# Opening a fused attention and feed-forward kernel in quarters instead of halves

## Chip, cores, metric

One core of one Trainium2 chip. The metric is the device time of one execution in microseconds (us).

## The reference, cut to what matters

```python
mod = (silu(c) @ w_mod).reshape(1, 6, 1, 1024)
sa, ca, ga, sb, cb, gb = (mod[:, i] for i in range(6))
h = layernorm(x) * (1 + ca) + sa                 # x: 2048 tokens x 1024
x = x + ga * attention(h, k_cache, v_cache, wq, wo)   # 32 query heads of 128
h = layernorm(x) * (1 + cb) + sb
x = x + gb * swiglu(h, w_gate, w_up, w_down)
```

The opening computes `q = h @ wq` for the first heads and the first 512 tokens. It needs the *scale columns* (the part of `w_mod` that gives `ca`, 2 MB), the first 512 columns of `wq` (four heads, 1 MB), and 512 normalised tokens, transposed. The shift `sa` enters later, as a bias on `q`.

## The kernel before: the parts concerned

P = 128, DT = 8 contraction tiles, HK = 4, CH = 512 tokens. Every load goes through SyncE's queue in this order:

```python
def load_wca(hf):                      # scale columns, one half: rows of 512 columns = 1024 B
    for i in range(4):
        SP.dma_start(wca[hf][:, 2*i:2*i+2, :], w_mod[2*i*P:(2*i+2)*P, D+hf*512:D+(hf+1)*512] ...)
for hf in range(2):
    load_wca(hf)
    load_wq0(hf)                       # first weights, half of the contraction
load_wq(1)                             # second group of weights (heads 4 to 7), 1 MB
load_k(0); ...shift columns...; load_v(0); load_wq(2)
load_x(1)                              # second 512 tokens, one load of 1 MB
```

The first heads, by halves of the contraction and of the tokens, with scale matmuls (`mod_ca`, one column each) and scaling out of PSUM (`x_mod`) between them:

```python
for kc in range(HK):
    for h in range(3):
        q_first(h, kc, 0, 2 * P)       # 256 tokens
    ...                                # transposes, x_mod, scale matmuls of half 1, other 256 tokens
for kc in range(HK, DT):
    for h in range(4):
        q_first(h, kc, 0, CH)
for h in range(4): q_raw(h)            # to SBUF
qproj_mm(4, QB0[4], 0, DT)             # fifth head: needs the second group of weights
```

Later, in the first turns of attention (`QB`, bank 4, is also the projection's bank; `XB`, bank 7, is free there):

```python
if i == 1: scores(0)
if i in (1, 3, 5): q_bias_mm(i + 1, i + 3, QB)   # ends with a copy out of the bank on VectorE
if i % 2 == 0: qproj(NQ0 - 1 + i // 2)           # writes bank QB
```

In the same turns ScalarE runs exponentials and, between them, statistics of the second 512 tokens (`stats_act`).

The softmax here doesn't subtract the row's maximum and nothing guards it: scores larger than these inputs give would overflow.

## Time and profile before

| | before |
|---|---|
| three runs | 1158.01, 1158.25, 1160.08 |
| span of the profiled run | 1156.8 |
| TensorE busy | 1145.8 (99%) |
| first projection starts | 11.29 |
| second group of weights lands, 15 engines / all 16 | 18.71 / 20.09 |
| fifth head starts | 20.14 |
| second exponential pair starts | 33.78 |

A load is spread over 16 DMA engines and counts as landed when the last has reported. "15 engines" is the landing without the slowest one. The two can differ by more than a microsecond here.

### The profile page before, as it was taken

The numbers are of one execution on the slowest core, as the hardware profiler recorded it, in microseconds if no ns is written. First come the engines' busy times: TensorE is split into PE (matmuls) and PEld (weight loads), VectorE is DVE, ScalarE is ACT, GpSimd is POOL, SyncE is SP. The second block draws the span as 40 slices with busy tenths as digits, with TensorE's granted clock in tenths as the row PEclk, the third lists the DMA queues.
The fourth block names the chain that finished last, engine by engine and source line by source line (L and its number), as shares of the span: only waits on it lengthen the run. The fifth ranks groups of instructions, "written<-read, shape, count | busy, mean of one in ns | idle before, by whom it ended". The sixth has DMA issues, their size and how long they took to land.

```text
span 1156.8 us, 18111 instructions
## 1 busy us (share of the span) xinstructions
PE 1145.8 (99%) x7029; PEld 585.5 (51%) x7029; DVE 825.1 (71%) x1651; ACT 532.0 (46%) x745; POOL 67.6 (6%) x137
## 2 busy tenths in 40 slices
PE   8999999999999999999999999999999999999999
PEld 5555656654446566656444444444444444444444
DVE  4777997747667777786657898777558777776536
ACT  3867787720127777787100354454110444444110
POOL 1100231000000111111000010000000000000000
DMA  9789899986808898945764332423874423234443
GB/s 321 135 178 216 214 211 207 239 188 180 238 16 186 205 209 212 205 96 126 195 198 151 94 88 73 110 74 100 209 206 140 119 76 107 73 98 131 131 159 109
DMA packets 298532, 179.96 MB, mean 156 GB/s; under 512 B 140496, under 2 KB 287696, under 8 KB 298448
## 3 DMA queue, kind: packets, MB, share of 16 engines
q1 hardware_dynamic: 235472, 92.31, 37.3%
q10 hardware_dynamic: 54336, 55.05, 15.2%
q0 software_dynamic: 8640, 31.46, 8.6%
q8 instruction: 55, 0.90, 0.3%
q14 instruction: 29, 0.24, 0.1%
HBM read 125.96 MB, written 19.92 MB: 126 GB/s over the span
## 4 chain that ended last, share of the span: by engine, by line
PE 93%; DMA 2%; DVE 2%; issue 1%; ACT 1%; SPq 1%; DVEq 0%; ACTq 0%
PE ps L272 93%; DMA arena<-in_A_wq_dram 1%; DMA arena<-nsc 1%; DVE arena L826 1%; ACT arena L796 1%; DMA arena<-arena 1%; DVE arena L897 0%; SPq L341 0%; DVE arena L1053 0%; DVE st L417 0%; SPq L310 0%; SPq L359 0%; DVE arena L843 0%; DVE nsc L431 0%; DVE arena L1552 0%
## 5 line engine op out<-in xcount | busy, mean ns | idle before, releaser
L272 PE MATMUL ps<-arena 128*128 128x512 f16 (+2 forms) x6800 | 1140.4, 330 | 7.9 <-POOL arena L410 2.2
L272 PEld LDWEIGHTS ps<-arena 128*128 128x128 bf16 (+1 forms) x6800 | 577.8, 98 | 564.5 <-DVE arena L826 7.0
L796 ACT ACTIVATE arena<-ps 128x1024 bf16<-128x1024 f32 x256 | 261.2, 1021 | 43.7 <-PE ps L272 31.9
L829 ACT ACTIVATE tmp<-ps 128x512 f32<-128x512 f32 x167 | 99.7, 597 | 295.5 <-PE ps L272 284.6
L897 DVE TENSOR_TENSOR arena<-arena 128x512 f16<-128x512 bf16 x328 | 133.1, 418 | 3.0
L826 DVE TENSOR_TENSOR arena<-ps,tmp 128x512 bf16<-128x512 f32 (+1 forms) x134 | 91.7, 685 | 50.7 <-PE ps L272 37.8
L829 ACT ACTIVATE nsc<-ps 128x512 f32<-128x512 f32 x84 | 50.1, 596 | 93.2 <-PE ps L272 90.9
L818 DVE TENSOR_TENSOR arena<-ps,rl 128x512 f16<-128x512 f32 x128 | 88.5, 691 | 5.1 <-DVE rl L815 0.7
L826 DVE TENSOR_TENSOR arena<-ps,nsc 128x512 f16<-128x512 f32 x84 | 57.3, 686 | 41.0 <-PE ps L272 29.7
L815 DVE RECIPROCAL rl<-ps 128x4 f32<-128x4 f32 x128 | 23.0, 180 | 75.6 <-PE ps L272 74.8
L1113 DVE TENSOR_TENSOR tmp<-ps,tmp 128x512 f32<-128x512 f32 x32 | 22.0, 689 | 61.0 <-ACT tmp L829 51.4
L1537 ACT ACTIVATE arena<-arena 128x512 f16<-128x512 f16 x84 | 49.9, 624 | 32.7 <-DVE arena L826 32.7
L1037 DVE TENSOR_TENSOR arena<-arena 128x2048 f16<-128x2048 f16 (+3 forms) x56 | 56.0, 1010 | 9.3 <-PE ps L272 8.8
L829 ACT ACTIVATE arena<-ps 128x512 f32<-128x512 f32 x16 | 9.6, 597 | 90.7 <-PE ps L272 90.7
L947 DVE TENSOR_TENSOR arena<-arena 128x512 f16<-128x512 bf16 x120 | 47.8, 419 | 1.4 <-DMA arena<-in_A_wo_dram 0.4
L417 DVE BATCH_NORM_STATS2 st<-x_res 128x6 f32<-128x512 bf16 x58 | 39.5, 682 | 3.7 <-DMA x_res<-in_A_x_dram 3.4
L594 DVE SCALAR_TENSOR_TENSOR arena<-arena 128x1024 bf16<-128x1024 bf16 x32 | 38.9, 1215 | 0.0
L1552 DVE TENSOR_TENSOR arena<-arena 128x512 f16<-128x512 f16 x84 | 35.0, 416 | 0.3
L1114 DVE TENSOR_TENSOR tmp<-tmp,rowb 128x512 f32<-128x512 f32 (+1 forms) x49 | 33.6, 686 | 1.7
L431 DVE TENSOR_SCALAR nsc<-x_res,mv,rstd 128x1024 f16<-128x1024 bf16 (+1 forms) x30 | 16.2, 538 | 22.3 <-DMA arena<-nsc 21.0
L1115 DVE TENSOR_TENSOR arena<-tmp,x_res 128x512 bf16<-128x512 f32 (+1 forms) x33 | 22.3, 676 | 1.1
L826 DVE TENSOR_TENSOR arena<-ps,rowb 128x512 f16<-128x512 f32 x28 | 19.3, 689 | 3.9 <-ACT rowb L829 3.4
(85 smaller groups left out, 325.6 us busy)
## 6 DMA issues: line engine op xcount, KB each, us to landing
arena<-in_A_wq_dram SPq DMA_DIRECT2D x28, 512.0 KB, 5.1
arena<-wo_sum ACTq DMA_DIRECT2D x7, 2048.0 KB, 8.8
arena<-in_B_w_gate_dram SPq DMA_DIRECT2D x28, 512.0 KB, 4.0
arena<-in_B_w_up_dram SPq DMA_DIRECT2D x28, 512.0 KB, 5.1
arena<-wd_sum ACTq DMA_DIRECT2D x8, 1792.0 KB, 7.8
arena<-in_B_w_down_dram ACTq DMA_DIRECT2D x6, 1792.0 KB, 7.2
arena<-in_A_wo_dram POOLq DMA_DIRECT2D x16, 512.0 KB, 4.9
wo_sum<-arena POOLq DMA_DIRECT2D x16, 512.0 KB, 5.0
```

The costliest lines, as they stand in the source:

```text
L272: T.op(PE, lambda: TE.matmul(out_ap, lhsT, rhs, start=start, stop=stop, skip_group_check=skip), reads=reads, writes=[bank_buf])
L417: T.op(DVE, lambda: V.bn_stats(st_[sl][:, hf * 6:hf * 6 + 6], x_res[:, t, hf * 512:hf * 512 + 512]), reads=[B_x[t]], writes=[B_st[sl]])
L594: T.op(DVE, lambda: V.scalar_tensor_tensor(mt[n % 2], mt[n % 2], 1.0, sc_row, op0=ALU.mult, op1=ALU.mult, accum_out=mcol[:, n:n + 1]), rea ...
L796: T.op(ACT, lambda: A.activation(ex_s[es][:, 2 * kp:2 * kp + 2, :], banks2(SCB + 2 * kp), AF.Exp, scale=att_scale), writes=[PB[SCB + 2 * k ...
L818: T.op(DVE, lambda: V.tensor_tensor(o_s[os_].rearrange("p (a b) d -> p a b d", a=2), psap(PVB * 512, [[512, 2], [130, 2], [1, P]]), rlb, A ...
L826: T.op(DVE, lambda: V.tensor_tensor(out, bank(ba), other, ADD), reads=[ob2], writes=[PB[ba], ob])
L829: T.op(ACT, lambda: A.activation(dst, bank(bk), AF.Copy), writes=[PB[bk], db])
L897: T.op(st, lambda: eng.tensor_tensor(o, a, b, op), reads=rd, writes=[wr])
L947: T.op(DVE, lambda: V.tensor_tensor(o, a, b, SUB), reads=rd, writes=[wr])
L1037: T.op(DVE, lambda: V.tensor_tensor(o, a, b, SUB), reads=rd, writes=[sb])
L1537: T.op(ACT, lambda: A.activation(o, s_, AF.Silu), reads=[sb], writes=[ob])
L1552: T.op(DVE, lambda: V.tensor_tensor(gu[blk][:, p, :], o, s_, MULT), reads=[sb, ob], writes=[B_gu[blk][p]])
```

## The change

Intent: start TensorE's useful work sooner. Scale columns and first weights come two contraction tiles at a time, all four heads take each quarter at once, and each token half gets its own PSUM bank. One later line moves the bias columns to the spare bank.

```diff
-            def load_wca(hf):
-                for i in range(4):
-                    T.op(dq("q_wca%d_%d" % (hf, i)), lambda: SP.dma_start(
-                        wca[hf][:, 2 * i:2 * i + 2, :],
-                        w_mod[2 * i * P:(2 * i + 2) * P, D + hf * 512:D + (hf + 1) * 512] ...
+            def load_wca(q):
+                parts = 2 if q == 0 else 1
+                m = DT // parts
+                for i in range(parts):
+                    T.op(dq("q_wca%d_%d" % (q, i)), lambda: SP.dma_start(
+                        wca[q][:, i * m:(i + 1) * m, :],
+                        w_mod[i * m * P:(i + 1) * m * P, D + q * 2 * P:D + (q + 1) * 2 * P] ...
...
-            for hf in range(2):
-                load_wca(hf)
-                load_wq0(hf)
+            for q in range(NQR):
+                load_wca(q)
+                load_wq0(q)
...
+            def x_place(t, dt):
+                if dt < HK:
+                    return t // 2, dt * 2 * P + t % 2 * P
+                return (0 if dt % 2 else 2), (dt - HK) // 2 * CH + t * P
...
-            warm(12, WB)
+            warm(10, WB)
...
+            q_four(0, 0, 2 * P)
+            mod_ca(1)
+            x_gain(1)
+            x_mod(1, 0, B_hT[0])
+            x_first(2, range(HK))
+            x_first(tl, range(HK))
+            x_mod(0, 2, B_h0b)
+            q_four(1, 0, 2 * P)
...
+            q_four(2, 0, CH)
+            q_four(3, 0, CH)
...
-                    q_bias_mm(i + 1, i + 3, QB)
+                    q_bias_mm(i + 1, i + 3, XB)
```

More of the change, by code (lines that the diff above doesn't have):

```diff
@@ L333, in _ @@
             ND = 12
-            B_wca = [[_Buf("wca%d_%d" % (hf, i)) for i in range(4)] for hf in range(2)]
+            NQR = DT // 2
+            B_wca = [[_Buf("wca%d_%d" % (q, i)) for i in range(2)] for q in range(NQR)]
             B_wsa = [_Buf("wsa%d" % k) for k in range(DT)]
-            wca = [arena.at(OFF_OT[2] + hf * 8 * KB, [DT, 512], BF16, B_wca[hf]) for hf in range(2)]
+            wca = [arena.at(OFF_OT[2] + q * 4 * KB, [DT, 2 * P], BF16, B_wca[q]) for q in range(NQR)]
             wsa = arena.at(OFF_OT[3], [DT, D], BF16, B_wsa)
-            def load_wca(hf):
-                for i in range(4):
-                    T.op(dq("q_wca%d_%d" % (hf, i)), lambda: SP.dma_start(
-                        wca[hf][:, 2 * i:2 * i + 2, :],
-                        w_mod[2 * i * P:(2 * i + 2) * P, D + hf * 512:D + (hf + 1) * 512].rearrange("(k p) n -> p k n", p=P)),
-                         writes=[B_wca[hf][i]])
+            def load_wca(q):
[4 more added lines that the diff above has]
+                        wca[q][:, i * m:(i + 1) * m, :],
+                        w_mod[i * m * P:(i + 1) * m * P, D + q * 2 * P:D + (q + 1) * 2 * P].rearrange("(k p) n -> p k n", p=P)),
+                         writes=[B_wca[q][i]] if parts == 2 else B_wca[q])
             NWQ = 2
@@ L356, in load_wq, with load_wq0 @@
                     wq_s[gidx], A_wq[:, gidx * 512:(gidx + 1) * 512].rearrange("(k p) n -> p k n", p=P)), writes=B_wq[gidx])
-            def load_wq0(kh):
-                T.op(dq("q_wq0%d" % kh), lambda: SP.dma_start(
-                    wq_s[0][:, kh * HK:(kh + 1) * HK, :],
-                    A_wq[kh * HK * P:(kh + 1) * HK * P, 0:512].rearrange("(k p) n -> p k n", p=P)), writes=[B_wq[0][kh]])
+            B_wq0 = [_Buf("wq0_%d" % q) for q in range(NQR)]
+            def load_wq0(q):
+                T.op(dq("q_wq0%d" % q), lambda: SP.dma_start(
+                    wq_s[0][:, 2 * q:2 * q + 2, :],
+                    A_wq[2 * q * P:(2 * q + 2) * P, 0:512].rearrange("(k p) n -> p k n", p=P)), writes=[B_wq0[q]])
             def load_wsa(k2):
@@ L490, in warm @@
                     mm(bank(b), zwarm[:, 0:P], zwarm, True, True, [B_zw], PB[b])
-            def x_first(t, d0=0, n=DT):
-                for dt in range(d0, d0 + n):
-                    o = (dt % 2) * CH + t * P
-                    transpose(bank_bf(dt // 2)[:, o:o + P], nsc4[t][:, dt * P:(dt + 1) * P], [B_ns4[t]], PB[dt // 2])
-            def x_gain(hf):
-                T.op(DVE, lambda: V.tensor_scalar(gain_f[:, hf * HK:(hf + 1) * HK], psap(XB * 512, [[2, HK]]), 1.0, None, op0=ALU.add),
-                     writes=[PB[XB], B_g[0]])
@@ L503, in x_mod @@
-            def x_mod(hf, c0, n, bufs):
-                for dt in (0, 2, 1, 3):
-                    dt += hf * HK
-                    src = bank_bf(dt // 2)[:, (dt % 2) * CH + c0:(dt % 2) * CH + c0 + n]
-                    dst = hT[0][:, dt, c0:c0 + n]
-                    if dt % 4 < 2:
+            B_gq = [_Buf("gq%d" % q) for q in range(NQR)]
+            def x_place(t, dt):
+                if dt < HK:
+                    return t // 2, dt * 2 * P + t % 2 * P
+                return (0 if dt % 2 else 2), (dt - HK) // 2 * CH + t * P
@@ new lines, in x_first, with x_gain, x_mod @@
+            def x_first(t, dts):
+                for dt in dts:
+                    bk, o = x_place(t, dt)
+                    transpose(bank_bf(bk)[:, o:o + P], nsc4[t][:, dt * P:(dt + 1) * P], [B_ns4[t]], PB[bk])
+            def x_gain(q):
+                T.op(DVE, lambda: V.tensor_scalar(gain_f[:, 2 * q:2 * q + 2], psap(XB * 512, [[2, 2]]), 1.0, None, op0=ALU.add),
+                     writes=[PB[XB], B_gq[q]])
+            def x_mod(q, t, bufs):
+                n = 2 * P if q < 2 else CH
+                for dt in (2 * q, 2 * q + 1):
+                    bk, o = x_place(t, dt)
+                    src = bank_bf(bk)[:, o:o + n]
+                    dst = hT[0][:, dt, t * P:t * P + n]
+                    if (t if q < 2 else dt % 2) == 0:
@@ L509, in x_mod @@
                         T.op(DVE, lambda: V.tensor_scalar(dst, src, gain_f[:, dt:dt + 1], None, op0=ALU.mult),
-                             reads=[B_g[0]], writes=[PB[dt // 2], bufs[dt]])
+                             reads=[B_gq[q]], writes=[PB[bk], bufs[dt]])
                     else:
                         T.op(ACT, lambda: A.activation(dst, src, AF.Copy, scale=gain_f[:, dt:dt + 1]),
-                             reads=[B_g[0]], writes=[PB[dt // 2], bufs[dt]])
+                             reads=[B_gq[q]], writes=[PB[bk], bufs[dt]])
@@ L515, in _, with mod_ca @@
             MCOLS = [(j, j) for j in range(DT)]
-            def mod_ca(hf, k):
-                mod_mm(wca[hf][:, k, :], B_wca[hf][k // 2], k, MCOLS[0:HK])
+            def mod_ca(q, k0=0, k1=DT):
+                for k in range(k0, k1):
+                    mod_mm(wca[q][:, k, :], B_wca[q][k // HK], k, MCOLS[0:2])
             WB = PVB
@@ L555, in _ @@
             norm(0, 0, 0)
-            stats_only(2)
+            stats(2, 2, 0)
+            norm(1, 1, 1)
+            stats(2, 2, 1)
+            T.op(DVE, lambda: V.bn_aggr(mv[2][:, :], st_[2][:, :]), reads=[B_st[2]], writes=[B_mv[2]])
             rstd_of(2, mv[2][:, 1:2], B_mv[2], 1.0)
             rstd_of(tl, acc[:, 1:2], B_acc, 1.0 / D)
-            norm(1, 1, 1)
-            norm(2, 2, 2, 0, 512)
-            warm(12, WB)
-            x_first(0)
-            warm(3, WB)
-            for k in range(4):
-                mod_ca(0, k)
-            x_first(1)
-            for k in range(4, DT):
-                mod_ca(0, k)
-                if k == 5:
-                    warm(1, WB)
-            x_first(2, 0, HK)
-            x_gain(0)
-            x_mod(0, 0, 2 * P, B_hT[0])
-            norm_last(0, 512)
-            norm(2, 2, 2, 512, 512)
+            warm(10, WB)
+            x_first(0, range(HK))
+            warm(2, WB)
+            mod_ca(0, 0, HK)
+            warm(1, WB)
+            x_first(1, range(HK))
+            mod_ca(0, HK, DT)
+            x_gain(0)
+            x_mod(0, 0, B_hT[0])
+            x_first(0, (4, 6))
+            x_first(1, (4, 6))
+            norm(2, 2, 2)
+            norm_last(0, D)
             NL = NJ - NE
@@ L653, in _ @@
             BB = SCB + 3
-            QB0 = [QB, PVB, PVB + 1, SCB, SCB + 1, SCB + 2, QB, PVB]
+            QB0 = [QB, PVB, PVB + 1, SCB + 3, SCB + 1, SCB + 2, QB, PVB]
             def q_raw(h):
@@ L696, in q_first @@
                 mm(bank(QB0[h], n, c0), wq_s[0][:, kc, h * P:(h + 1) * P], hT[0][:, kc, c0:c0 + n],
-                   kc == 0 and c0 == 0, kc == DT - 1, [B_wq[0][kc // HK], bufs[kc]], PB[QB0[h]], skip=True)
-            for kc in range(HK):
-                for h in range(3):
-                    q_first(h, kc, 0, 2 * P)
-                if kc == 2:
-                    x_first(tl, 0, HK)
-                    x_mod(0, 2 * P, 2 * P, B_h0b)
-                    norm_last(512, 512)
-            for k in range(4):
-                mod_ca(1, k)
@@ L708, in _ @@
-            x_first(2, HK, HK)
-            for kc in range(HK):
-                for h in range(3):
-                    q_first(h, kc, 2 * P, 2 * P, B_h0b)
-                if kc == 1:
-                    x_first(tl, HK, HK)
-                    for k in range(4, DT):
-                        mod_ca(1, k)
-                    x_gain(1)
-                    x_mod(1, 0, CH, B_hT[0])
-            for kc in range(HK):
-                q_first(3, kc, 0, CH)
-            for kc in range(HK, DT):
-                for h in range(4):
-                    q_first(h, kc, 0, CH)
+                   kc == 0 and c0 == 0, kc == DT - 1, [B_wq0[kc // 2], bufs[kc]], PB[QB0[h]], skip=True)
@@ new lines, in q_four @@
+            def q_four(q, c0, n, bufs=B_hT[0]):
+                for kc in (2 * q, 2 * q + 1):
+                    for h in range(4):
+                        q_first(h, kc, c0, n, bufs)
+            q_four(0, 0, 2 * P)
[6 more added lines that the diff above has]
+            q_four(1, 0, 2 * P)
+            x_mod(1, 2, B_h0b)
+            q_four(0, 2 * P, 2 * P, B_h0b)
@@ L723, in _ @@
+            mod_ca(2)
+            x_gain(2)
+            for t in range(2, TPC):
+                x_first(t, (4, 6))
+            for t in range(TPC):
+                x_first(t, (5, 7))
+            x_mod(2, 0, B_hT[0])
+            q_four(1, 2 * P, 2 * P, B_h0b)
+            mod_ca(3)
+            x_gain(3)
+            x_mod(3, 0, B_hT[0])
+            q_four(2, 0, CH)
+            q_four(3, 0, CH)
             for h in range(4):
                 q_raw(h)
-            T.op(DVE, lambda: V.tensor_copy(gain[0][:, :], gain_f[:, :]), writes=[B_g[0]])
+            T.op(DVE, lambda: V.tensor_copy(gain[0][:, :], gain_f[:, :]), reads=B_gq, writes=[B_g[0]])
```

## The prediction

> **What bounds the kernel now.** I read the page first (busy shares, then the chain that ended last), then the chain and each engine's order of time over the first 60 us, since every changed line but one runs before 20 us, and the last one before 43 us.
>
> ```profile
> PE 1145.8 (99%) x7029; PEld 585.5 (51%) x7029; DVE 825.1 (71%) x1651; ACT 532.0 (46%) x745; POOL 67.6 (6%) x137
> PE 93%; DMA 2%; DVE 2%; issue 1%; ACT 1%; SPq 1%; DVEq 0%; ACTq 0%
> ```
>
> TensorE is busy for 99% and carries 93% of the chain. Its idle time in the whole run is 1156.8 - 1145.8 = 11.0 us, 0.95% of the span, so no opening of any shape gains 2% by removing waits. The chain over the stretch that changes:
>
> ```profile
> 8.60 11.49 DMA arena<-in_A_wq_dram
> 20.09 0.05 issue
> 20.14 2.28 PE ps L272 x24
> ...
> 29.50 1.60 PE ps L272 x20
> 31.10 0.02 issue
> 31.12 0.17 DVE bq L668
> 31.29 0.14 issue
> 31.43 3.44 PE ps L272 x24
> 34.87 0.03 issue
> 34.90 1.03 ACT arena L796
> ```
>
> Columns are start, length, what. Until 20.09 us the chain is not TensorE at all: it is the DMA queue, and its last link is the landing of the second group of query weights (1 MB, issued at 8.60, landed 20.09). From there it is TensorE, with a small detour over VectorE at 31.12 and exponentials on ScalarE later. TensorE's own order of time says how near the two limits lie:
>
> ```profile
> 11.29 1.16 PE L272 MATMUL ps<-arena 128*128 128x256 f16 x9 [0.65 <-DMA arena<-in_A_wq_dram]
> 20.14 1.90 PE L272 MATMUL ps<-arena 128*128 128x512 f16 x8 [0.27 <-DMA arena<-in_A_wq_dram]
> 31.43 1.24 PE L272 MATMUL ps<-arena 128*128 128x512 f16 x5 [0.51 <-DVE bq L668]
> ```
>
> The brackets are idle time before the group and what ended it. The first heads' matmuls start at 11.29, after 0.65 us for the weights' first half; their last one could have been followed by another at about 19.7 (the row before ends at a modelled 19.87), and then TensorE waits for the second group until 20.14. The last line is a separate wait, taken up below.
>
> **The Trainium skill.** "DMA: Bandwidth & Descriptors", Specifications, puts the smallest transfer for line rate at 512 B. The change cuts the scale columns' rows from 1024 B to 512 B, so this matters. This trace has both sizes in saturated stretches of one microsecond; the last number is GB/s:
>
> ```profile
> 10.00:11.00 1.00, 0.64 (x13) 0.37 (x10) 0.70 (x3) 0.26 (x1) 0.58 (x1) 1.00 1.07 358
> 12.00:13.00 1.00, 1.00 (x19) 0.93 (x17) 0.40 (x3) 0.29 (x1) 0.00 (x0) 1.00 1.10 353
> 955.00:956.00 1.00, 1.00 (x6) 0.44 (x5) 0.97 (x4) 0.60 (x1) 0.00 (x0) 1.00 1.15 346
> ```
>
> The first two move 1024 B packets, the third 512 B packets (gate weights): 346 against 353 and 358, so it agrees nearly, with a few per cent lost. "Runtime: NRT & Kernel Launch", Instruction fetch mechanics, says that a sequencer fetches its own program in 16 KiB blocks of 256 instructions by its own DMA queue. The trace agrees: the page's
>
> ```profile
> q8 instruction: 55, 0.90, 0.3%
> ```
>
> is 55 packets of 16384 B, and TensorE's 14,058 weight loads and matmuls make 54.9 blocks of 256. "PSUM — Partial Sum Buffer", bank collisions, says two engines may not touch one bank at once, so programs guard by bank and not by address; this kernel's waits do that, as the 0.51 us above shows: the next projection and the two bias columns being copied lie in one bank. "TensorE: Matmul & The Clock Gate" gives a floor of about 25 ns from start to start for small matmuls; the 16 one-column matmuls at 12.83 start 25 ns apart, so splitting them by quarters costs nothing as long as their number stays.
>
> **The change part by part.**
>
> *Loads ahead of the second group.* Bytes are equal: tokens 1 MB, scale columns 2 MB, first weights 1 MB. Only their order and the 512 B rows differ. First matmul: before, 1 MB of scale columns and 0.5 MB of weights had to land (11.24); now 0.5 and 0.25 MB. The last tokens landed at 6.69 and a 256 KB piece took about 0.75 us, so three pieces are in at about 9.0, some 2 us earlier. The second group's landing cannot profit, since the same bytes are queued before it: 2.10 MB at 340 instead of 355 GB/s is 6.17 - 5.91 = 0.26 us later.
>
> That landing has a second part. In the trace 15 of its 16 engines' completions were in by 18.71 and the last at 20.09: one DMA engine is 1.38 us late in everything from then on. At 15.75 a 16 KB instruction block (1127 ns) was fetched, when TensorE had started 141 matmuls. In the new order the 141st falls in the last quarter's scale matmuls (my count: 128 before them), about 16.2, still before the group has drained. So I expect the same lateness: 20.09 + 0.26 = about 20.35.
>
> *TensorE's work to the first four heads.* Transposes 32 both times; scale matmuls 64 both; projections 24 of 256 columns and 20 of 512 become 32 and 16, the same columns (16,384, at 216 ns per 512: 6.9 us); warming matmuls 18 become 15 in all. I walked the new order with durations of this trace (statistics 0.69, normalising 0.49, 256 columns from PSUM 0.35 on VectorE and 0.48 on ScalarE, 512 columns 0.48 and 0.69, power on POOL 0.55): second normalisation 8.2 instead of 8.97; first gain 9.3; first projection 9.8; two gaps, about 0.7 us before it and 0.35 at 11.8 for the second quarter's scaling behind the normalisations on VectorE; from 12.1 on no gap; ready for the fifth head at about 19.7. That is what it was before: the early start is eaten by doing one quarter at a time, each with its chain of scale matmuls, gain and scaling. Readiness at 19.7 is hidden behind 20.35.
>
> *Banks in the opening.* Tokens of each half in their own bank let ScalarE and VectorE read without the other half's transposes waiting. All this lies before 19.7: worth nothing at the end while the weights land later.
>
> *The bias columns to the spare bank.* This is on the path after the landing. Before: the bias matmuls end about 30.92, VectorE copies them 31.12 to 31.28, TensorE starts the projection into the same bank at 31.43, 0.51 idle. Now the projection goes to another bank and starts at 30.93. Its fifth step needs VectorE's shifts, ready 31.54, 31.80, 32.07, 32.33, and reaches them at 31.79, 32.00, 32.22, 32.44: just in time. Then scores, then the exponential at 33.78, before which ScalarE was idle 0.47 us waiting for TensorE. ScalarE is free from 33.32, so 0.46 of the 0.50 is kept. From 34.90 TensorE waits for those exponentials, so all moves forward by 0.46. The two later uses (34.9 and 40.8) show no wait now, so nothing there.
>
> Sum: +0.26 (landing) - 0.46 (bank) = -0.20, to 1158.05.
>
> **Rivals.** *The fetch misses the transfer, or falls elsewhere.* Then the group lands at 18.97 and TensorE's readiness at 19.7 sets the end: -0.4 -0.46, to 1157.4. For it: the position by count is only known to some ten matmuls. Against it: nearly 3 us would have to be missed. *TensorE becomes later than the weights.* From 12.1 on my walk has no slack, so a late VectorE or POOL (0.55 to 0.6 per power) shifts the end one to one; 1 us late gives 20.7 and 1158.4. *The 512 B rows cost more*, as they do by packet durations taken alone (27 against 46 ns for half the bytes): 256 x 27 - 128 x 46 = 1.0 us per engine, giving 1158.8. Against it: the saturated rates above. *The author's intention comes true*, opening shorter by the 1.5 us by which projections start earlier: 1156.7. The DMA chain speaks against it.
>
> **Range and chances.** Weighing the four rivals (the first a quarter, the second a quarter, the third a sixth) moves the middle slightly below the sum, to 1157.9. The three runs before span 1158.01 to 1160.08, so noise adds mostly upward. Range 1156.8 to 1159.3. Two per cent is 23 us, against 11 us of all TensorE idle; nothing here adds 23 us either, since the opening's whole changed part lasts 20. Chances: faster 0.01, within 0.98, slower 0.01.
>
> **What would show it.** Right: first projection before 10.5; the chain still ends its DMA part with the second weights, landing 20.0 to 20.8, and TensorE idle for them more than the 0.27 of now; the wait on the bias copy gone; the exponential after it about 0.46 earlier relative to that landing. Wrong: the chain before 20 us running over VectorE, ScalarE or the scale columns; the landing before 19.5 or after 21; the 0.51 us coming back at 31.5 as a wait for the shifts.

## More of the kernel before

The runs of one call share a chip. The second of the three later calls (spare bank again, later fetch, fewer warming matmuls, the change again) ran on another chip than the other two; the chip of the first comparison is not on record.

## The result, and the profile after

Six runs of the changed kernel: median 1159.30 (1158.65 to 1161.53). Six of the kernel before beside them: 1159.05 (1158.01 to 1160.13). The ratio is 1.0005, 95% interval 0.9992 to 1.0017: no difference that the runs resolve. A ratio here is the mean time of one kernel's fast runs over that of the other's in the same rounds, so it is not quite the ratio of the medians.

The chain of work that ended last, changed kernel (start, length, what):

```profile
12.12 8.64 DMA arena<-in_A_wq_dram
20.75 0.05 issue
20.80 2.28 PE ps L272 x24
...
30.39 5.18 PE ps L272 x63
35.56 1.01 ACT arena L811
```

The DMA part still ends with the second group of weights, now at 20.75 instead of 20.09. The detour over the copy of the bias columns at 31.12 is gone; in one run from 30.39 TensorE works to the exponentials. And yet the exponential at the end of it is at 35.56 (34.90 before), as late as the weights were. TensorE's order of time says the same (the last figure in brackets is the idle time and its cause):

```profile
10.30 1.03 PE L272 MATMUL ps<-arena 128*128 128x256 f16 x8 [0.58 <-DVE arena L521]
20.80 1.90 PE L272 MATMUL ps<-arena 128*128 128x512 f16 x8 [0.49 <-DMA arena<-in_A_wq_dram]
31.44 3.77 PE L272 MATMUL ps<-arena 128*128 128x512 f16 x28
```

The first projection starts 1 us earlier, the fifth head 0.66 later, and the projection that waited for the bias copy now starts at 31.44 (31.43 before) with no wait. So the spare bank bought back the lost 0.66, and within the next 4 us that gain was gone again. ScalarE's order of time tells where. Before:

```profile
32.18 1.05 ACT L730 ACTIVATE tmp<-x_res 128x1024 bf16<-128x1024 bf16 x1
33.78 2.14 ACT L796 ACTIVATE arena<-ps 128x1024 bf16<-128x1024 f32 x2 [0.47 <-PE ps L272]
```

After:

```profile
33.40 1.06 ACT L745 ACTIVATE tmp<-x_res 128x1024 bf16<-128x1024 bf16 x1 [0.45 <-DMA x_res<-in_A_x_dram]
34.45 2.12 ACT L811 ACTIVATE arena<-ps 128x1024 bf16<-128x1024 f32 x2
```

Before, ScalarE had its statistics done and waited for TensorE's scores. Now it waits for the second 512 tokens, which landed at 33.37 instead of 32.09, does the statistics, and only then the exponentials that TensorE needs.

How the difference goes on can be read exactly. The two programs issue the same TensorE instructions after the opening, so I matched the k-th last weight load of one trace with the k-th last of the other and took the difference of their starts, after minus before: +0.66 at 22 us, +0.01 at 31.6, +0.65 at 36.5, +0.65 at 120, +0.66 at 250, +0.24 at 280, +0.23 at the end. Two hundred microseconds of attention carry the shift unchanged to two hundredths. Then one place alters it: transposed activations that land behind a 2 MB load of summed output weights. The chain there, before:

```profile
252.97 9.40 DMA arena<-nsc
262.37 0.03 issue
...
266.52 23.48 PE ps L272 x108
```

After:

```profile
255.75 6.86 DMA arena<-nsc
262.61 0.03 issue
...
266.76 23.27 PE ps L272 x107
```

TensorE goes on 0.24 later there, not 0.65. This place is DMA-paced, and over the runs below it altered the shift by -0.9 to +0.2.

### The profile page after: what moved, and what is told of

Its sections match the earlier page's. It is cut to its first block, busy times and chain, and to the rows that moved or that the text cites. A ratio compares the mean times of both kernels' runs of the same rounds, so it can differ in the third digit from the quotient of the medians.

```text
span 1157.0 us, 18031 instructions
## 1 busy us (share of the span) xinstructions
PE 1141.0 (99%) x6946; PEld 585.9 (51%) x7030; DVE 825.2 (71%) x1651; ACT 532.1 (46%) x745; POOL 69.2 (6%) x137
## 4 chain that ended last, share of the span: by engine, by line
PE 92%; DVE 2%; DMA 2%; issue 1%; ACT 1%; SPq 1%; DVEq 0%; ACTq 0%
PE ps L272 92%; ACT arena L811 1%; DMA arena<-in_A_wq_dram 1%; DMA arena<-arena 1%; DMA arena<-nsc 1%; SPq L364 1%; DVE arena L841 1%; DVE arena L912 0%; SPq L344 0%; DVE arena L1068 0%; DVE st L422 0%; SPq L310 0%; DVE arena L858 0%; DVE nsc L436 0%; DVE arena L1567 0%
```

## The experiments

My theory after the comparison had three parts. (1) Rows of 512 B are slower than I allowed and hold up the second group of weights. (2) A 16 KB block of TensorE's own program, fetched during that transfer, makes one DMA engine late. (3) The spare bank is worth half a microsecond, unless ScalarE has to wait for the second tokens. The rivals: the order of the loads, not their rows, makes the weights late; the spare bank is worth nothing; the slow engine has another reason. Totals scatter by more than these sums, so the traces decide. The readings of all runs, shift against the first profile of before in us:

| kernel | 15 / 16 engines | shift at 22 | at 31.6 | at 36.5 | at 280 |
|---|---|---|---|---|---|
| before | 18.71 / 20.09 | 0 | 0 | 0 | 0 |
| change | 19.80 / 20.75 | +0.66 | +0.01 | +0.65 | +0.24 |
| change, again | 20.66 / 20.76 | +0.67 | +0.02 | +0.13 | +5.68 |
| change, third | 19.79 / 20.85 | +0.76 | +0.11 | +0.23 | +4.66 |
| change without spare bank | 19.77 / 21.42 | +1.33 | +1.34 | +1.34 | +1.15 |
| change, rows of 1024 B | 18.94 / 19.89 | +0.45 | -0.20 | -0.09 | +0.32 |
| change, tokens in four loads | 19.85 / 21.31 | +1.22 | +0.57 | +0.68 | +0.31 |
| before, rows of 512 B | 19.51 / 20.69 | +0.60 | +0.60 | +0.60 | +4.58 |
| before + spare bank, again | 18.31 / 19.55 | -0.08 | -0.73 | -0.62 | -1.10 |
| before + spare bank, third | 18.97 / 19.75 | -0.18 | -0.83 | -0.71 | -1.21 |
| before, fewer scale matmuls | 19.02 / 19.57 | -0.44 | -0.44 | -0.44 | +4.01 |
| before + bank, fewer warming | 18.74 / 18.85 | +1.00 | +0.35 | +0.47 | +4.12 |

### Spare bank alone, first try

```diff
-                    q_bias_mm(i + 1, i + 3, QB)
+                    q_bias_mm(i + 1, i + 3, XB)
```

> The kernel before with only the bias columns moved to the spare bank. Theory: before the change nothing but TensorE's wait stood ahead of the second pair of exponentials (ScalarE idle 0.47 us there), so with the token load unchanged the whole shortening arrives: second group of weights lands at about 20.1 as before, the 0.51 us wait at 31.4 is gone, the exponential that started at 33.78 starts at 33.3 to 33.4, and TensorE's instructions from 36 to 250 us start 0.4 to 0.5 us earlier than before. Rival: the bank is worth nothing by itself (the shifts on VectorE take its place): exponential still at 33.8, shift 0. The total moves at most 0.5 us either way, which three rounds will not resolve.

The profile fell on an execution of 1722 us at a granted clock of 0.655 and says nothing about waits. Its three other runs: 1157.22 to 1158.21; ratio 0.9987, interval 0.997 to 1.0003. It was run again (below).

### Rows of 512 B alone

The kernel before, with the same eight loads of 256 KB, but each of four contraction tiles and 256 columns (the scale matmuls wait for their loads accordingly; those lines are left out):

```diff
-                        wca[hf][:, 2 * i:2 * i + 2, :],
-                        w_mod[2 * i * P:(2 * i + 2) * P, D + hf * 512:D + (hf + 1) * 512]
+                        wca[hf][:, k0:k0 + HK, c0:c0 + 256],
+                        w_mod[k0 * P:(k0 + HK) * P, D + hf * 512 + c0:D + hf * 512 + c0 + 256]
```

> The kernel before with only the rows of the scale columns halved to 512 B (same bytes, same number of loads). Theory (rows of 512 B run at about 28 ns a packet, not at 340 GB/s): 15 of the 16 engines land the second group at 19.7 to 19.9 instead of 18.71, the fifth head starts at 20.7 to 21.2, and TensorE stays 0.6 to 1.1 us later from there to 250 us. Rival (the order of the new loads or the new order of issue makes them late, not the rows): 18.7 and 20.1 as before.

15 engines at 19.51 (somewhat less than expected), all at 20.69, shift +0.60: nearly the whole +0.66 of the change, with its order of loads and of work left out. For 15 engines it is 0.80 of the change's 1.09. One profile of each can't settle the rest, but over all usable profiles the rows divide the landings: with 1024 B rows 15 engines were in at 18.31 to 19.02 (six profiles), with 512 B rows at 19.51 to 20.66 (six). The stretches in which the scale columns alone land, in this kernel (the last number is GB/s):

```profile
6.43:9.92 3.49, 3.06 (x42) 1.96 (x39) 2.60 (x7) 2.39 (x4) 2.09 (x6) 1.00 1.14 310
11.48:15.04 3.56, 3.39 (x48) 2.98 (x48) 1.94 (x6) 1.45 (x4) 0.00 (x0) 1.00 1.19 301
```

and the second of them in the kernel before:

```profile
11.24:14.24 3.00, 2.95 (x45) 2.75 (x46) 1.81 (x6) 1.42 (x3) 0.00 (x0) 1.00 1.09 350
```

The same megabyte takes 3.56 us instead of 3.00. The total (median 1160.28, ratio 1.0013, interval 0.9994 to 1.0032) does not resolve it.

### The change with rows of 1024 B

```diff
-            for q in range(NQR):
-                load_wca(q)
-                load_wq0(q)
+            for hf in range(2):
+                load_wca(hf)               # two loads of 512 KB, rows of 512 columns
+                load_wq0(2 * hf)
+                load_wq0(2 * hf + 1)
```

> The changed kernel with the scale columns loaded in halves with 1024 B rows again, the work still in quarters. Theory: 15 engines land the second group at 18.6 to 18.9 (19.80 in the change), all 16 by 19.6 to 20.1; then TensorE itself is the limit, ready at about 20.2 to 20.6 since its first projections start later (10.8 to 11.2), so the fifth head starts at 20.2 to 20.6 instead of 20.80. Rival (order of loads): 19.8 and 20.75 stay.

As expected: 15 engines at 18.94, all at 19.89. Now TensorE is the limit. Its last sixteen projections start at 17.14 and follow each other at 0.216, so it is ready at about 20.6, and the shift at 22 is +0.45:

```profile
10.73 1.05 PE L272 MATMUL ps<-arena 128*128 128x256 f16 x8 [0.63 <-DMA arena<-in_A_wq_dram]
17.14 4.69 PE L272 MATMUL ps<-arena 128*128 128x512 f16 x21
```

This +0.45 isn't the price of the quarters alone: with the scale columns in halves again the first projections start at 10.73, after a wait for weights, and not at 10.30 as in the change. In the change itself TensorE was ready at 20.0 to 20.6; with the opening in halves it was at about 19.7, or 20.06 in a run without any wait for the weights (spare bank, again). So no run shows the quarters ready earlier than the halves, and most show them later. Median 1158.90, ratio 0.9994 (0.9976 to 1.0012).

### The change with the second tokens in four loads

```diff
-            load_x(1)
+            for t in (TPC, TPC + 2, TPC + 1, TPC + 3):
+                T.op(dq("q_xs%d" % t), lambda: SP.dma_start(x_res[:, t, :], xf[t * P:(t + 1) * P, :]), writes=[B_x[t]])
```

> The changed kernel with the load of the second 512 tokens cut into four loads of 256 KB, first those that the statistics read first. Theory: the gain of the spare bank was given back because ScalarE's statistics wait for these tokens (0.45 us, until 33.37). Now the first tile lands two microseconds earlier, the wait is gone, the exponential of 34.45 starts at 33.95 to 34.1 (the scores are then ready), and TensorE's shift against before from 36 to 250 us is +0.2 to +0.3 instead of +0.65, if the weights land as in the change (20.75). Rival (ScalarE or VectorE is simply full there): exponential stays at 34.4, shift +0.65.

The weights landed later than in the change (21.31, one engine 1.46 behind), so the absolute numbers of the expectation do not hold. The first tokens land at 31.44, and ScalarE's statistics start without a wait,

```profile
31.36 2.14 ACT L812 ACTIVATE arena<-ps 128x1024 bf16<-128x1024 f32 x2
33.40 1.05 ACT L746 ACTIVATE tmp<-x_res 128x1024 bf16<-128x1024 bf16 x1
34.47 2.14 ACT L812 ACTIVATE arena<-ps 128x1024 bf16<-128x1024 f32 x2
```

and the shift goes from +1.22 at 22 us to +0.68 at 36.5: 0.54 of the spare bank is kept although everything was later. But the run doesn't test the mechanism: ScalarE was free for the statistics only at 33.40, and in a run about as late (the change without spare bank, below) tokens in one load were there at 33.40 too. The test is in the three profiles of the change itself. Median 1158.72, ratio 0.9995 (0.998 to 1.001).

### Spare bank alone, again

> The same kernel as the first run (before, with only the bias columns in the spare bank), because that profile fell on an execution with a granted clock of 0.655 and tells nothing of the waits. Expected as written there: fifth head at about 20.1, no wait at 31.4, exponential at 33.3 to 33.4 instead of 33.78, TensorE 0.4 to 0.5 us earlier than before from 36 to 235 us. If ScalarE's or VectorE's work fills the gap instead, the exponential stays at 33.8. At the end of the kernel I expect less than 0.3 us of it, because in the runs so far a chain of transposes behind the 2 MB load of summed output weights lands at 262.4 to 262.7 whatever the opening did.

Measured: -0.08 at 22, -0.62 at 36.5, so 0.54 from the bank. The exponential starts at 33.16, with ScalarE busy before it:

```profile
32.10 1.05 ACT L730 ACTIVATE tmp<-x_res 128x1024 bf16<-128x1024 bf16 x1
33.05 0.19 ACT L730 ACTIVATION_READ_ACCUMULATOR tmp<-x_res 128x1 f32 x1
33.16 2.14 ACT L796 ACTIVATE arena<-ps 128x1024 bf16<-128x1024 f32 x2
```

My expectation for the end was wrong: the shift grew to -1.10 behind the junction at 262 instead of shrinking, so that place does not simply absorb. Median 1157.86, ratio 0.999 (0.9978 to 1.0002).

### A later fetch of the program

The last three of eight steps of the scale matmuls left out. Its output is wrong, which doesn't matter for the time. It was run on another chip. (The check of the result passed it all the same.)

```diff
-                mod_mm(wca[hf][:, k, :], B_wca[hf][k // 2], k, MCOLS[0:HK])
+                if k < 5:
+                    mod_mm(wca[hf][:, k, :], B_wca[hf][k // 2], k, MCOLS[0:HK])
```

> Wrong result on purpose: the kernel before without the last three of eight contraction steps of the scale columns, 24 one-column matmuls (0.6 us of TensorE) fewer ahead of the second group of weights. TensorE's 16 KB program block was fetched when 141 matmuls had started, at 15.75; now that number falls behind the first four heads. Theory (the fetch holds one of the 16 DMA engines and with it every later landing): no fetch before 18.7, all 16 engines land the second group at 18.6 to 18.9 instead of 20.09, the fifth head starts at 19.0 to 19.3 without a DMA wait. Rival (one engine is late for another reason, for example its share of the bytes): 15 engines at 18.7, the last near 20.1, fetch or no fetch.

The experiment missed its aim. The block was fetched at 17.16, when 123 matmuls had started, not when the 141st had: the fetch is not tied to what TensorE has started. It still fell into the transfer, and the last engine was 0.55 behind the fifteenth. It decides nothing between theory and rival by itself; it refutes my rule for when the fetch comes. Counted with the matmuls left out, it came at 123 + 24 = 147, and in the next run at 130 + 12 = 142, inside the 139 to 148 of the ten other profiles: it may follow the place in the program and not the number. No run tests that. Median 1159.07, ratio 1.0006 (0.9991 to 1.0021).

What the landings say of the rival: a share of bytes that makes one engine slow should show in every load. In the load just before, the last quarter or half of the first weights, the last engine was 0.03 to 0.41 behind the fifteenth in all twelve usable profiles. In ten of them the lag then jumps in the load under way at the fetch, to 0.55 to 1.65. So a standing cause is unlikely. Two things stay open: a landing doesn't name its engine, so that the late one is the one that fetched is inferred; and the lag was in five profiles longer than the 1.1 us that the block took.

### Fewer warming matmuls

```diff
-            warm(12, WB)
+            warm(4, WB)
-            warm(3, WB)
...
-                if k == 5:
-                    warm(1, WB)
-                    q_bias_mm(i + 1, i + 3, QB)
+                    q_bias_mm(i + 1, i + 3, XB)
```

> A version that may beat both, correct: before, with the spare bank and 12 warming matmuls fewer (12 to 4, and the 3 and 1 between the first transposes), so that the fetch comes 12 matmuls later, at about 18, when nearly all of the second group has been read. Theory: last engine at 18.7 to 19.4, fifth head at 19.7 to 19.8 (TensorE itself), exponential at 32.9 to 33.0, TensorE 0.7 to 0.9 us earlier than before up to 235 us. Rival: without the warming matmuls TensorE runs at its slow start rate in the transposes and first projections (one 512-column matmul per 0.43 us, as the first five do now) and the fifth head starts later than 20.5.

It was run on another chip. Both sides were half right. The fetch came at 17.33 and left the second group alone: all 16 engines at 18.85. In the next loads the last engine was then behind: by 0.55 in the first keys, by 0.60 in the first shift columns (20.53 and 21.13). So one engine falls behind from about the fetch on, and which load that delays seems to depend on when it comes; the run before had its fetch only 0.17 earlier, and there the second group was delayed. But TensorE was slow. Nine matmuls of 256 columns, with the wait before them, in this kernel:

```profile
11.37 2.09 PE L272 MATMUL ps<-arena 128*128 128x256 f16 x9 [0.43 <-DMA arena<-in_A_wq_dram]
```

They took 1.16 before. The fifth head came 1.0 us late although its weights came early. Median 1160.90, ratio 1.0018 (1.0003 to 1.0032), the only interval that excludes 1, on the slower side.

### The change, again

> The changed kernel once more, to see how far one profile can be trusted. If the readings are of the kernel and not of one execution: 15 engines at 19.7 to 19.9, all at 20.6 to 21.4 (the lateness of the engine with the fetch was 0.89 to 1.46 in six runs), statistics on ScalarE waiting for the tokens until about 33.4, exponential at 34.3 to 34.6, shift against before +0.5 to +0.7 up to 235 us and less than 0.5 after 266.

+0.67 at 22 again, and +0.13 at 36.5: here the second tokens landed at 32.76, ScalarE did not wait, and the spare bank's 0.54 was kept:

```profile
32.85 1.05 ACT L745 ACTIVATE tmp<-x_res 128x1024 bf16<-128x1024 bf16 x1
33.91 2.14 ACT L811 ACTIVATE arena<-ps 128x1024 bf16<-128x1024 f32 x2
```

Fifteen engines were at 20.66 this time, because several engines lagged, not one. The expectation of 33.4 for the tokens was wrong; the first profile of the change was the odd one. In that first profile the second group of weights was not later (20.75). The load just ahead of the tokens (the third group of weights) was: its last two engines landed at 30.13 and 30.91, against 30.06 and 30.13 in this one. Why is open; a block of the program was fetched within that load in all three profiles of the change (at 28.58 to 28.67). At the end the new profile was 5.7 us late all the same, from a slip between 200 and 250 us. Waits of TensorE's weight loads, and of VectorE, in that stretch of this kernel (total, times, longest):

```profile
PEld ps L272 <- DVE arena L841: 4.1, 2, 4.0
```

```profile
DVE arena L962 <- DMA arena<-in_A_wo_dram: 4.1, 1, 4.1
```

VectorE waits 4 us for a block of output weights that is loaded, summed and stored in the background, and TensorE waits for VectorE. That is 4 of the 6.0 us lost there; the rest wasn't traced. Five of the twelve usable profiles stand 4 us or more late at 280 us, and they do not go by kind of kernel: two of the three of the change, and those of the kernel before with 512 B rows, with fewer scale matmuls (there between 120 and 150 us already), and with the bank and fewer warming matmuls. Single runs of the unaltered kernel before reach 1164.75 too. In all five VectorE waited 3.1 us or more in one go for such a block in the stretch of the slip; in the first profiles of before and of the change it did not. Slips of this size are as large as the scatter of the totals (1157.75 to 1164.75 for the kernel before), and so probably make up much of it. What starts one stays open.

### All three

The change without the spare bank (`XB` back to `QB` in the one line), the spare bank alone, and the change:

> The changed kernel with the bias columns back in the projection's bank, so the opening in quarters alone. Theory (the opening costs about 0.65 us and the spare bank gains about 0.54, unless the tokens land after about 32.9): shift of TensorE against before +0.5 to +0.8 at 22 us, the same at 31.6 with the 0.51 us wait there again, the same from 36 to 120. In the total it should be the slowest of the three of this call, by 0.3 to 0.8 us over the change, which five rounds may just not resolve. Rival (the spare bank does nothing in the changed kernel, as its first profile suggested): no difference to the change at 36 us, but then both at +0.65.

> The kernel before with the spare bank alone once more, beside the change on the same chip. Theory: shift against before between -0.7 and -0.4 from 36 to 120 us, the total 0.5 to 1.3 us below before (two measurements so far: 0.13 and 0.10%), so the fastest of the three. Rival: the two measurements were chance, and it is within 0.3 us of before.

> The changed kernel a third time. Two profiles gave +0.66 and +0.67 at 22 us, then +0.65 and +0.13 at 36.5, the difference being the landing of the second tokens (33.37 and 32.76). Theory: +0.5 to +0.9 at 22; at 36.5 about 0.54 less if these tokens land before 32.9, and less of a reduction the later they land, none from 33.4. The total within 0.1% of before.

Without the spare bank the shift stays as it starts, +1.33, +1.34, +1.34, and the wait is back:

```profile
32.76 0.59 PE L272 MATMUL ps<-arena 128*128 128x512 f16 x2 [0.51 <-DVE bq L679]
```

It starts at +1.33 rather than the expected 0.5 to 0.8 because the last engine was 1.65 behind; 15 engines were at 19.77 as in the change. The tokens landed at 33.40 and cost nothing there, since ScalarE had to wait for the scores anyway. Spare bank alone: -0.18, then -0.71. The change: +0.76, then +0.23, tokens at 32.79. Medians 1159.87, 1157.97 and 1159.58; ratios 1.0006 (0.9982 to 1.003), 0.999 (0.9966 to 1.0013) and 1.0003 (0.998 to 1.0026).

So the version that looks best is the kernel before with one line changed. Three calls gave 0.9987, 0.999 and 0.999; each interval alone includes 1, so the totals don't prove it; the traces show its 0.54 at 36.5 us. Over all its 13 fast runs the median is 1157.86, against 1158.82 over the 35 runs of before and 1159.58 over the 16 of the change.

## Why the prediction was wrong

**The bound, and the class.** Right. TensorE's 99% leaves nothing near 2%, and the change measured 1.0005 of before (at most 1.0017 by the interval). The DMA part of the chain ended with the second group of weights in all three traces of the change.

**The failing step: "2.10 MB at 340 instead of 355 GB/s is 6.17 - 5.91 = 0.26 us later".** Measured, 15 engines were 1.09 later in the change (19.80 against 18.71) and 0.80 later with the rows alone. I had read the rate of 512 B packets from single microseconds that I picked because they were full of them (346 GB/s in another stage). The landing of whole megabytes ran at 301 and 310. So the term of the sum that was mis-sized is the landing: +0.26 stood for what measured +0.80 to +1.09. My third rival, the packet durations taken alone, gave 1.0 us and came close; I dismissed it with the picked windows. (It took 27 ns for a packet of 512 B, as in the picked microsecond; in the two megabytes above they took 30 and 34 ns.) Why the gate weights of that stage were faster in their best microsecond is not settled; I chose the fastest.

**"So I expect the same lateness".** The slow engine was 1.38 behind in before, and 0.95, 0.10 and 1.06 in the three profiles of the change. It varies from run to run (up to 1.65), and that, with +1.09, makes the net +0.66 in the first profile: 1.09 - 0.43. So it was luck that the landing, at 20.75, fell inside the 20.0 to 20.8 that I had named as a sign of being right; the first projection before 10.5, the longer wait for the weights (0.49) and the vanished bias wait came true as well, and none of them could tell the sum from its opposite. The sign that could, the exponential 0.46 earlier relative to the landing, failed in the first profile (13.70 after it, 13.69 in before) and came true in the two others (13.15 and 13.16). That the fetch causes the lag is supported by the landings before and after it and by the run in which the second group escaped, but not shown; how its moment is set stays open, and my count to the 141st matmul is not it.

**"Ready for the fifth head at about 19.7".** Measured: 20.0 to 20.6 in the three profiles, from the start of the last sixteen projections (16.54 to 17.10) and 0.216 each. My walk had the first projection at 9.8 and no gap after 12.1; it started at 9.87 to 10.30, and in the second profile 0.37 went to a wait for scale columns at 11.6. Hidden behind the weights, as said; but in the run with long rows, which started its projections later still, TensorE's readiness came to light as +0.45. So my second rival was partly true as well.

**"0.46 of the 0.50 is kept".** The size was right: 0.53 or 0.54 in seven traces with the spare bank (two of the change, two of the bank alone, long rows, tokens in four loads, fewer warming matmuls), nothing in those without it. I had named the shifts on VectorE as what could take its place. What took it in the first profile of the change was another wait, for the second tokens, which had landed 0.6 later than in the two others. In those two nothing took it.

**The sum.** I had +0.26 - 0.46. In the traces it is +0.7 - 0.54, and nothing of the 0.54 in the profile whose tokens came at 33.37. The end then moves by what the transposes at 262 us do, and by the background slips.

**The level.** The first three runs of before gave 1158.25, all 35 give 1158.82, and the six beside the change 1159.05. I placed the sum on the three; the measured 1159.30 lies at the very upper edge of the range. Of the 1.25 between it and the sum's 1158.05, 0.80 is this level (1159.05 - 1158.25) and 0.45 is the difference to before, +0.25 in place of -0.20; and no run resolves that difference in the totals.

## What to carry to other kernels

When a transfer sets the path, splitting it so that the first piece comes sooner can make its last piece later; cost the row length by the time that whole loads of that row length take to land, not by the fullest microsecond of another stage. Follow a removed wait to the next engine and ask what that engine's other inputs are: here ScalarE's wait for its tokens, 0.45 us, took the place of the 0.47 us that had been removed. And where one small line among a large rewrite carries the gain, try that line alone.

## What the Trainium skill lacked or had wrong

- "DMA: Bandwidth & Descriptors", Specifications: 512 B as the smallest transfer for line rate. In these runs one megabyte of 512 B rows landed in 3.49 to 3.56 us and one of 1024 B rows in 3.00, so line rate was not reached at 512 B; 2048 B rows took 1.36 us for half a megabyte.
- "Runtime: NRT & Kernel Launch", Instruction fetch mechanics: the cost of crossing a block boundary is called "mostly hidden". Here the 16 KB block took about 1.1 us of one DMA engine, and the last engine to land the load under way was 0.55 to 1.65 us behind the fifteenth in ten of the twelve usable profiles (0.10 and 0.11 in the other two, one with several slow engines, one whose next loads were late instead). That the fetch is the cause is inferred. The page speaks of the sequencer's side only.
- No page says at which point of the running block the next one is fetched. Here 123 to 148 matmuls had started when the first fetch seen began, over the twelve usable profiles.
